# Own PSUM banks for two key and two query transposes, a third transpose buffer, a lag of three for the first eight units, and no steps put off

## The chip, the cores and the metric

One Trainium2 chip, of which one core runs the whole program. The metric is device time in microseconds (us) of one execution, the median of several executions. The engines are named as in the profile: PE (TensorE matmuls), PEld (TensorE weight loads), DVE (VectorE), ACT (ScalarE), POOL (GpSimd) and SP (SyncE, which here only issues transfers).

## What is computed

Attention with a position bias for 4 batches, 8 heads, 576 positions and a head size of 64, followed by a feed-forward block on the 2304 tokens (model size 512, hidden size 2048). Cut to what matters:

```python
scores = q @ k.transpose(0, 1, 3, 2) / sqrt(D)
psi_rel = log1p(abs(pos[:, None] - pos[None, :])); psi_i = log1p(maximum(pos[:, None], 1))
h = maximum((psi_rel / psi_i)[..., None] @ w1 + b1, 0.0)      # 32 hidden values per pair of positions
scores = scores + (h @ w2).transpose(2, 0, 1)[None]           # one bias for each head
attn = exp(scores - max(scores)); attn = attn / (sum(attn) + 1e-09)
x = (attn @ v).transpose(0, 2, 1, 3).reshape(B * S, H * D)
h = x @ w_in
out = (h / (1.0 + exp(-1.702 * h))) @ w_out
```

## The kernel before, in words

Every product of f32 operands is made of f16 halves: each operand is split into a high and a low part, and three products (high by high, high by low, low by high) are added in PSUM. The split of an operand is an ACT copy (high part) and a DVE or POOL subtraction (low part).

The attention runs in 72 units. A unit is one batch `b`, one chunk `c` of 128 query positions (the fifth chunk has 64) and one pair of heads `hp`. For unit `u` the main loop (line 655) writes down, in this order:

- `emit_s(u)`: the score products of both heads into one four-bank PSUM tile of the pool `ps_s` (line 329).
- `emit_soft1(u)`: bias added and maximum taken on DVE (line 352), exponential on ACT (line 359), split into `hl` (lines 364 to 367), and one transposing transfer `aT<-hl` on SP's queue (line 373). `a32` and `hl` have two buffers each, the target `aT` has two of tag `aT` for units up to 28.
- some steps of the feed-forward block, `msteps` (line 666).
- `emit_av(u - AV_LAG)`: the products of the transposed attention with V for an earlier unit, into a one-bank tile of the pool `ps_h` (line 392), then the scaling `xf` and split `xn`, and after the last head pair of a chunk the transposing transfer `xT<-xn` (line 426).
- weight conversions (`W_STEPS`, up to three per unit until all 32 are done), the first half of a bias step, more steps of the feed-forward block (line 667), the second half of the bias step, the bias load of unit `u + 2`, and what `todo` holds for the unit: loads, query transposes `trans_q`, key transposes `trans_k`, V splits.

`ps_s` has one buffer of four banks: score tiles, the tiles of `trans_q` (line 244), of `trans_k` (line 271) and of some bias steps follow one another in it. `ps_h` has two buffers of one bank, shared by `emit_av` and the first feed-forward product `hp` (line 488). `ps_o` has two buffers of one bank.

The feed-forward block works on ten blocks of tokens (both batches of a chunk; 256 tokens, or 128 for the fifth chunk), 16 steps each. A step is `emit_m1` (12 matmuls `hp<-xT,wi`, line 496, then ACT, DVE and POOL work) and, two steps behind, `emit_m2` (6 matmuls `op<-wo,gT`, line 525). A block's steps may be written down once the last of its units has had its `emit_av`; for the first block that is unit 10 of the loop. A unit has one step ahead of `emit_av` (`STEPS_A`) and one behind it (`STEPS_B`), except that `STEPS_B` is 0 in units 13, 15, 17, 19, 21 and 23. What is left is done after the loop (line 676).

The order written down is a priority, not the final order: a planner simulates the program at build time, and on each engine a step that is not ready in that simulation is passed by later ones. On the chip each engine and each transfer queue then works strictly in the order so found.

At the start, the last 64 key positions of batches 0 and 1 are loaded into two buffers of tag `xT` (lines 607 and 609), which later hold the transposed blocks `xT`.

Of the kernel before, what the change touches and what calls it, by code (L numbers as in the profile page):

```python
# [7 lines left out]
F32 = mybir.dt.float32  # L8
F16 = mybir.dt.float16
U32 = mybir.dt.uint32  # L10
ACTF = mybir.ActivationFunctionType
# [9 lines left out]
def kernel(  # L21
# [26 lines left out]
    nc = tc.nc  # L48
    B, H, S, D = q.shape
# [3 lines left out]
    NF = DFF // 128  # L53
    NP = H // 2
    SM = 512
    ST = S - SM
    BS = 512.0
    KS = 8.0
# [21 lines left out]

    W_AHEAD = 3
    BIAS_AHEAD = 2
    AV_LAG = 2
    STEPS_A = {}
    STEPS_B = {u: 0 for u in (13, 15, 17, 19, 21, 23)}
    W_STEPS = [1, 2, 2, 3, 3, 3, 3, 3, 3, 3, 3, 3]

    cst = ctx.enter_context(tc.tile_pool(name="cst", bufs=1))
# [2 lines left out]
    ps_s = ctx.enter_context(tc.tile_pool(name="ps_s", bufs=1, space=PSUM))  # L91
    ps_h = ctx.enter_context(tc.tile_pool(name="ps_h", bufs=2, space=PSUM))
# [4 lines left out]
    idn = cst.tile([128, 128], F32, name="idn")  # L97
# [17 lines left out]
    NU = len(units)  # L115
# [5 lines left out]
    for g in range(B // 2):  # L121
        b0, b1_ = 2 * g, 2 * g + 1
        for c in range(5):
            n = 128 if c < 4 else ST
# [3 lines left out]
    last_unit = [0] * len(blocks)  # L128
# [85 lines left out]
    q_st, k_st, kt_st, v_st = {}, {}, {}, {}  # L214
    qT, kT, v16 = {}, {}, {}

    def stage(shape, dt, tag, name):
        return wk.tile(shape, dt, tag=tag, name=name, bufs=BUFS[tag])

    def lo_part(on_pool, out, in0, scale, in1):  # L220
        if on_pool:
            nc.gpsimd.tensor_tensor(out=out, in0=in0, in1=in1, op=ALU.subtract)
        else:
            nc.vector.scalar_tensor_tensor(  # L224
                out=out, in0=in0, scalar=scale, in1=in1, op0=ALU.mult, op1=ALU.subtract
            )
# [11 lines left out]
        nc.sync.dma_start(out=t, in_=q[b, :, 128 * c:128 * c + n, :].rearrange("h p d -> p h d"))  # L238
        q_st[b, c] = t

    def trans_q(b, c):
        t = q_st.pop((b, c))
        n = t.shape[0]
        ps = ps_s.tile([128, 4, 512], F32, tag="s", name="qp")[:, 0, 0:NP * n]
        for hp in range(NP):
            nc.tensor.transpose(
                ps[:, n * hp:n * hp + n], t[:, 2 * hp:2 * hp + 2, :].rearrange("p a d -> p (a d)"), idn[:n, :n]
            )
        d = stage([128, 2, NP * 128], F16, "qT", "qT")[:, :, 0:NP * n]
        nc.scalar.activation(out=d[:, 0], in_=ps, func=ACTF.Copy, scale=QS)  # L250
        lo_part(False, d[:, 1], ps, QS, d[:, 0])
        qT[b, c] = d.rearrange("p x (u n) -> p x u n", u=NP)
# [16 lines left out]
    def trans_k(b, e):  # L269
        t = k_st[b, e]  # L270
        pair = ps_s.tile([128, 4, 512], F32, tag="s", name="kp").rearrange("p (u a) n -> p u (a n)", u=2)
        for u in range(2):
            ps, hp = pair[:, u, 0:S], 2 * e + u
            for c in range(4):
                nc.tensor.transpose(ps[:, 128 * c:128 * c + 128], t[:, u, c, :], idn)
            nc.tensor.transpose(ps[:, SM:S], kt_st[b][:, hp, :], idn[:ST, :ST])
            d = stage([128, 2, S], F16, "kT", "kT")
            nc.scalar.activation(out=d[:, 0], in_=ps, func=ACTF.Copy, scale=KS)
            lo_part(False, d[:, 1], ps, KS, d[:, 0])
            kT[b, hp] = d  # L280

    def load_v(b, e, tag="st"):

# [39 lines left out]
    s_ps, a_t, rs_t, aT = {}, {}, {}, {}  # L323
# [19 lines left out]
    def emit_soft1(u):  # L343
        bt = bt_t[u]
        at = wk.tile([128, 2 * S], F32, tag="a32", name="a32", bufs=BUFS["a32"])
        mx = wk.tile([128, 2], F32, tag="mx", name="mx")
        sm = wk.tile([128, 2], F32, tag="sm", name="sm", bufs=6)
        hl = wk.tile([128, 2, 2 * S], F16, tag="hl", name="hl", bufs=BUFS["hl"])
        for a in range(2):
            cs = slice(S * a, S * a + S)  # L350

            nc.vector.tensor_tensor_reduce(  # L352
                out=at[:, cs], in0=s_ps.pop((u, a))[:, 0:S], in1=bt[:, cs], scale=-1.0 / BS, scalar=3.0e38,
                op0=ALU.add, op1=ALU.min, accum_out=mx[:, a:a + 1],
            )
            nc.vector.tensor_scalar(  # L356
                out=mx[:, a:a + 1], in0=mx[:, a:a + 1], scalar1=LN_AS, scalar2=None, op0=ALU.add
            )
            nc.scalar.activation(  # L359
                out=at[:, cs], in_=at[:, cs], func=ACTF.Exp, scale=-1.0, bias=mx[:, a:a + 1],  # L360
                accum_out=sm[:, a:a + 1],
            )
            if a < VEC_EXP.get(u, 0):
                nc.vector.tensor_copy(hl[:, 0, cs], at[:, cs])
            else:
                nc.scalar.copy(hl[:, 0, cs], at[:, cs])  # L366
            (nc.vector if a and u in VEC_EXP_LO else nc.gpsimd).tensor_tensor(  # L367
                out=hl[:, 1, cs], in0=at[:, cs], in1=hl[:, 0, cs], op=ALU.subtract
            )
        rs_t[u] = sm  # L370

        t = stage([128, 18, 128], F16, "aT" if u <= max(BIAS_A) or u % 4 < 2 else "ht", "aT")
        nc.sync.dma_start_transpose(out=t, in_=hl.rearrange("p x n -> p (x n)"))
        aT[u] = t

    NXB = 2
    xT, x_n = {}, {}
# [97 lines left out]
    def weights_to(n):  # L475
        while w_done[1] < min(n, 2 * NF):
            split_w()
# [78 lines left out]
    def drain_to(j):  # L556
# [5 lines left out]
    FIRST = {1: (trans_k, 0, 0), 3: (trans_q, 0, 0)}  # L562
    SECOND = ((trans_q, 1, 0), (trans_k, 1, 0), (split_v, 0, 0))
    FIRST_UNITS = (
        (0, (load_k, 1, 1)), (1, (split_v, 1, 0)), (2, (trans_k, 0, 1)),
        (1, (load_v, 0, 1)), (4, (split_v, 0, 1)), (3, (load_v, 1, 1)),
        (4, (trans_k, 1, 1)), (6, (split_v, 1, 1)),
    )
    BIAS_A = {*range(4), *range(5, 21), 22, 24, 26, 28}
    BIAS_B = set(range(4))  # L570
# [2 lines left out]
    def at(u, fn, *args):  # L573
        todo.setdefault(u, []).append((fn, args))

    def put(us, items):
        assert len(us) == len(items)
        for u, x in zip(us, items):
            at(u, *x)
# [3 lines left out]
    for g in range(B // 2):  # L583
        b0, b1_ = 2 * g, 2 * g + 1
        o = g * UPG
        for c in range(4):
            put([o + 8 * c + x for x in (2, 5, 4, 7)], (
                (load_q, b0, c + 1), (trans_q, b0, c + 1), (load_q, b1_, c + 1), (trans_q, b1_, c + 1),
            ))
        if g + 1 < B // 2:  # L590
            n0, n1 = b0 + 2, b0 + 3
            for u, x in (
                (27, (load_kt, n0)), (28, (load_kt, n1)), (29, (load_k, n0, 0)), (30, (load_k, n1, 0)),
                (31, (load_v, n0, 0)), (32, (load_q, n0, 0)), (32, (trans_k, n0, 0)), 
                (32, (load_k, n0, 1)), (33, (load_q, n1, 0)), (33, (trans_k, n1, 0)), 
                (33, (load_k, n1, 1)), (33, (trans_q, n0, 0)), (34, (load_v, n1, 0)),
                (35, (split_v, n0, 0)), (35, (trans_q, n1, 0)), (35, (trans_k, n0, 1)),
                (36, (split_v, n1, 0)), (36, (load_v, n0, 1)), (36, (trans_k, n1, 1)), (37, (load_v, n1, 1)),
                (37, (split_v, n0, 1)), (38, (split_v, n1, 1)),
            ):  # L600
                at(o + u, *x)
# [12 lines left out]
        out=idn, in_=idn, compare_op=ALU.not_equal, fill=1.0, base=0, pattern=[[-1, 128]], channel_multiplier=1  # L614
# [16 lines left out]
    def bias_first():  # L631
        if bq:
            c, i = bq.pop(0)
            eng = BIAS_ENG[8 * c + i]
            half.append((c, i, eng, bias_hidden(c, i, eng, ("ht", "ht"))))

    def bias_second():
        if half:
            x = half.pop(0)
            bias_products(*x, "os")  # L640
            bdone[x[0]] += 1

    def bias_get(u):
        c = units[u][1]
        assert bdone[c] == (8 if c < 4 else 4)
        bias_load(u)

    def msteps(ready, n):
        n *= 256
        while n > 0 and fpos[0] < ready:  # L650
            n -= step()

    for u in range(BIAS_AHEAD):
        bias_get(u)
    for u in range(NU + AV_LAG):
        if u < NU:
            emit_s(u)
            emit_soft1(u)
        ready = NF * sum(1 for x in last_unit if x < u - AV_LAG)
        msteps(ready, STEPS_A.get(u, 1))  # L660
        if u >= AV_LAG:
            emit_av(u - AV_LAG)
        if u < len(W_STEPS):
            weights_to(w_done[1] + W_STEPS[u])
        if u in BIAS_A:
            bias_first()
        msteps(ready, STEPS_B.get(u, 1))
        bias_second()
        if u in BIAS_B:
            bias_first()  # L670
            bias_second()
        if u + BIAS_AHEAD < NU:
            bias_get(u + BIAS_AHEAD)
        for fn, args in todo.get(u, ()):
            fn(*args)
# [56 lines left out]
```

## Time and profile before

| what | value |
|---|---|
| median of 3 runs | 750.28 us (749.64 to 752.01) |
| the profiled execution's own time | 748.27 us |
| its span, first to last instruction | 746.4 us |
| mean granted TensorE clock | 0.93 of full speed |
| PE busy | 636.8 us (85% of the span) |
| DVE busy | 452.4 us (61%) |
| ACT busy | 421.2 us (56%) |
| POOL busy | 344.5 us (46%) |

The profile is of one execution; its span and the time around it (748.27 - 746.4 = 1.9 us) make its own time, which is 2.0 us under the median of the runs. Shares of busy time are means over stretches that have different limits, so the rows below are read stretch by stretch.

### The profile page before, as it was taken

To read this page: it belongs to the slowest core of one execution; us is meant where nothing else is said; L and a number is where in the kernel's file an instruction comes from. 1 tells how busy PE (TensorE), PEld (TensorE's weight loads), DVE (VectorE), ACT (ScalarE), POOL (GpSimd) and SP (SyncE) were. 2 spreads that over 40 slices of the span, in tenths; PEclk is the share of its full clock that TensorE was granted. 3 is DMA by queue.
4 is the path that set the end of the run, shared out by engine and by line. 5 is a ranking of instruction groups with operands and counts; after the bars stand their busy time and mean duration, and the time that the engine had idled before them with its cause. 6 is when DMAs were issued, how large, how long until landed. Compare 5 with 4: busy or idle time off the path is not lost.

```text
span 746.4 us, 17317 instructions
## 1 busy us (share of the span) xinstructions
PE 636.8 (85%) x6648; PEld 403.6 (54%) x6648; DVE 452.4 (61%) x1232; ACT 421.2 (56%) x971; POOL 344.5 (46%) x432
## 2 busy tenths in 40 slices
PE   5664763468988888999969899889999999999997
PEld 3222332235544555666647466566666666667665
DVE  6677769988556546645667566434676766642221
ACT  6899896577557745655445445763435454432133
POOL 2204634444445535655443465654474665552222
PEclk9778696569999999999998999999999999999999
DMA  9778989999867758877666676985467775752000
GB/s 241 227 256 233 289 189 220 259 239 242 184 148 144 171 104 168 170 153 145 145 145 144 154 137 124 199 160 117 86 135 145 160 143 124 143 102 54 1 29 15
DMA packets 249843, 116.50 MB, mean 156 GB/s; under 512 B 229792, under 2 KB 234016, under 8 KB 249760
## 3 DMA queue, kind: packets, MB, share of 16 engines
q1 hardware_dynamic: 241664, 99.38, 63.5%
q10 hardware_dynamic: 7952, 15.43, 5.9%
q8 instruction: 52, 0.85, 0.5%
q0 software_dynamic: 144, 0.59, 0.2%
q14 instruction: 31, 0.25, 0.1%
HBM read 52.85 MB, written 15.34 MB: 91 GB/s over the span
## 4 chain that ended last, share of the span: by engine, by line
PE 60%; DMA 14%; ACT 9%; DVE 9%; issue 4%; POOL 2%; SPq 1%; ACTq 0%; DVEq 0%; POOLq 0%
PE hp L496 22%; PE op L525 20%; DMA aT<-hl 11%; PE ot L404 7%; PE sp L336 5%; ACT a L359 3%; DVE a L352 3%; ACT ht L165 2%; PE ot L397 2%; POOL hl L367 2%; PE o L188 2%; ACT os L195 1%; DVE sm L388 1%; ACT hl L366 1%; ACT v L318 1%
## 5 line engine op out<-in xcount | busy, mean ns | idle before, releaser
L367 POOL TENSOR_TENSOR hl<-a,hl 128x576 f16<-128x576 f32 x142 | 189.1, 1344 | 123.0 <-ACT hl L366 59.6
L496 PE MATMUL hp<-xT,wi 128*128 128x256 f16 (+1 forms) x1920 | 219.5, 266 | 12.6 <-DMA xT<-xn 6.3
L525 PE MATMUL op<-wo,gT 128*128 128x512 f16 x864 | 216.8, 383 | 1.7 <-DVE gT L511 1.6
L496 PEld LDWEIGHTS <-wi 128*128 128x128 f16 x1920 | 170.5, 99 | 52.6 <-issue 16.9
L512 POOL TENSOR_TENSOR gT<-th,gT 128x256 f16<-128x256 f32 (+1 forms) x160 | 105.0, 657 | 165.1 <-DVE gT L511 89.8
L502 ACT ACTIVATE th<-hp 128x256 f32<-128x256 f32 (+1 forms) x160 | 57.2, 359 | 164.7 <-PE hp L496 156.0
L504 DVE SCALAR_TENSOR_TENSOR th<-th,hp 128x256 f32<-128x256 f32 (+1 forms) x160 | 62.4, 391 | 120.9 <-ACT th L502 120.9
L359 ACT ACTIVATE a<-a,mx 128x576 f32<-128x576 f32 x144 | 110.3, 768 | 42.2 <-DVE mx L356 41.8
L525 PEld LDWEIGHTS <-gT 128*128 128x128 f16 x864 | 81.0, 98 | 73.7 <-issue 3.9
L352 DVE CUSTOM_DVE_ANT_0 a<-sp,bt 128x576 f32<-128x576 f32 x144 | 103.1, 753 | 26.4 <-PE sp L336 22.6
L336 PE MATMUL sp<-kT,qT 64*128 64x512 f16 (+1 forms) x960 | 71.8, 297 | 13.7 <-DVE kT L224 3.6
L165 ACT ACTIVATE ht<-tab,pk 128x576 f32<-128x576 f32 x96 | 78.2, 863 | 5.8 <-PE ol L190 3.6
L404 PE MATMUL ot<-v,aT 128*128 128x64 f16 (+1 forms) x1920 | 78.8, 201 | 0.0
L404 PEld LDWEIGHTS <-aT 128*128 128x128 f16 (+1 forms) x1920 | 72.3, 106 | 3.7 <-issue 3.0
L366 ACT CAST hl<-a 128x576 f16<-128x576 f32 x103 | 66.0, 665 | 4.7 <-DMA aT<-hl 4.5
L419 POOL TENSOR_TENSOR xn<-xf,xn 128x128 f16<-128x128 f32 x72 | 35.4, 491 | 62.2 <-ACT xn L418 52.8
L397 PE MATMUL ot<-v,aT 128*128 128x128 f16 (+1 forms) x240 | 29.0, 233 | 39.1 <-DMA aT<-hl 39.0
L336 PEld LDWEIGHTS <-qT 64*128 64x128 f16 (+1 forms) x960 | 28.9, 99 | 56.5 <-issue 27.6
L388 DVE TENSOR_SCALAR sm<-sm 128x2 f32<-128x2 f32 x72 | 29.4, 408 | 35.9 <-ACT a L359 35.8
L188 PE MATMUL om<-ht,pk 128*32 128x512 f32 x152 | 41.5, 781 | 10.4 <-ACT os L195 10.4
L397 PEld LDWEIGHTS <-aT 128*128 128x128 f16 (+1 forms) x240 | 17.8, 104 | 58.0 <-DMA aT<-hl 47.0
L511 DVE CAST gT<-th 128x256 f16<-128x256 f32 x112 | 42.4, 379 | 4.4
(60 smaller groups left out, 562.9 us busy)
## 6 DMA issues: line engine op xcount, KB each, us to landing
bt<-scr SPq DMA_DIRECT2D x31, 576.0 KB, 4.4
scr<-os ACTq DMA_DIRECT2D x36, 288.0 KB, 4.1
w<-in_moe_w_in_dram SPq DMA_DIRECT2D x16, 512.0 KB, 5.3
w<-in_moe_w_out_dram SPq DMA_DIRECT2D x16, 512.0 KB, 5.2
k<-in_k_dram SPq DMA_DIRECT2D x32, 128.0 KB, 4.3
q<-in_q_dram SPq DMA_DIRECT2D x16, 256.0 KB, 4.8
out_dram<-ob ACTq DMA_DIRECT2D x16, 256.0 KB, 3.5
bt<-scr SPq DMA_DIRECT2D x8, 288.0 KB, 4.6
```

The costliest lines, as they stand in the source:

```text
L165: nc.scalar.activation(out=h, in_=tv, func=ACTF.Relu, bias=b1c, scale=sc[:, col:col + 1])
L336: nc.tensor.matmul(ps[a][64 * e:64 * e + m, cs], lhsT=qt[r, x, hp + e, 0:m], rhs=kT[b, hp + e][r, y, cs], start=i == 0, stop=i == 2,)
L352: nc.vector.tensor_tensor_reduce(out=at[:, cs], in0=s_ps.pop((u, a))[:, 0:S], in1=bt[:, cs], scale=-1.0 / BS, scalar=3.0e38, op0=ALU.add, ...
L359: nc.scalar.activation(out=at[:, cs], in_=at[:, cs], func=ACTF.Exp, scale=-1.0, bias=mx[:, a:a + 1], accum_out=sm[:, a:a + 1],)
L366: nc.scalar.copy(hl[:, 0, cs], at[:, cs])
L367: (nc.vector if a and u in VEC_EXP_LO else nc.gpsimd).tensor_tensor(out=hl[:, 1, cs], in0=at[:, cs], in1=hl[:, 0, cs], op=ALU.subtract)
L397: nc.tensor.matmul(o[po, 0:128], lhsT=t[:, 9 * y + 4, po], rhs=vt[:, x, 256:384], start=i == 0, stop=False, skip_group_check=True,)
L404: nc.tensor.matmul(o[po, 64 * a:64 * a + 64], lhsT=t[:, 9 * y + 5 * a + kb, po], rhs=vt[:, x, 384 * a + 64 * kb:384 * a + 64 * kb + 64], s ...
L496: nc.tensor.matmul(p[:, :n], lhsT=wi16[:, x, cc, 128 * f:128 * f + 128], rhs=r, start=i == 0, stop=i == 11,)
L504: nc.vector.scalar_tensor_tensor(out=g[:, :n], in0=th[:, :n], scalar=1.0, in1=p[:, :n], op0=ALU.add, op1=ALU.mult)
L512: nc.gpsimd.tensor_tensor(out=gt[:, 1, :n], in0=g[:, :n], in1=gt[:, 0, :n], op=ALU.subtract)
L525: nc.tensor.matmul(op_t[j, i], lhsT=gt[:, x, ts], rhs=wo16[:, f, y, :], start=f == 0 and n3 == 0, stop=f == NF - 1 and n3 == 2,)
```

## The change

`trans_q` gets a switch with which its tile comes from `ps_h` in place of `ps_s`; it is set for the two query transposes of units 5 and 7 (chunk 1, batches 0 and 1). A new function `trans_k_own` replaces `trans_k` in units 2 and 4 (head pairs 2 and 3 of batches 0 and 1): it transposes the last 64 key positions of both pairs first, into one `ps_h` tile, copies and splits them, and then handles each pair's other 512 positions in a `ps_h` tile of its own. The target of the attention's transposing transfer has the tag `xT` in units 2 and 5, so that three buffers serve the first units. The lag of `emit_av` is 3 in units 0 to 7 and 2 after that; unit 8 has two `emit_av` (5 and 6). `STEPS_B` is empty: units 13, 15, 17, 19, 21 and 23 have a step behind `emit_av` as well.

```diff
--- before.py
+++ after.py
@@ -80,9 +80,10 @@
 
     W_AHEAD = 3
     BIAS_AHEAD = 2
-    AV_LAG = 2
+    AV_LAG = {u: 3 for u in range(8)}
+    AT_X = {2, 5}
     STEPS_A = {}
-    STEPS_B = {u: 0 for u in (13, 15, 17, 19, 21, 23)}
+    STEPS_B = {}
     W_STEPS = [1, 2, 2, 3, 3, 3, 3, 3, 3, 3, 3, 3]
 
     cst = ctx.enter_context(tc.tile_pool(name="cst", bufs=1))
@@ -238,10 +239,14 @@
         nc.sync.dma_start(out=t, in_=q[b, :, 128 * c:128 * c + n, :].rearrange("h p d -> p h d"))
         q_st[b, c] = t
 
-    def trans_q(b, c):
+    def trans_q(b, c, own=False):
         t = q_st.pop((b, c))
         n = t.shape[0]
-        ps = ps_s.tile([128, 4, 512], F32, tag="s", name="qp")[:, 0, 0:NP * n]
+        if own:
+
+            ps = ps_h.tile([128, 512], F32, tag="h", name="qp")[:, 0:NP * n]
+        else:
+            ps = ps_s.tile([128, 4, 512], F32, tag="s", name="qp")[:, 0, 0:NP * n]
         for hp in range(NP):
             nc.tensor.transpose(
                 ps[:, n * hp:n * hp + n], t[:, 2 * hp:2 * hp + 2, :].rearrange("p a d -> p (a d)"), idn[:n, :n]
@@ -278,6 +283,28 @@
             nc.scalar.activation(out=d[:, 0], in_=ps, func=ACTF.Copy, scale=KS)
             lo_part(False, d[:, 1], ps, KS, d[:, 0])
             kT[b, hp] = d
+
+    def trans_k_own(b, e):
+
+        t = k_st[b, e]
+        tails = ps_h.tile([128, 512], F32, tag="h", name="kt")
+        ds = []
+        for u in range(2):
+            nc.tensor.transpose(tails[:, ST * u:ST * u + ST], kt_st[b][:, 2 * e + u, :], idn[:ST, :ST])
+        for u in range(2):
+            ds.append(stage([128, 2, S], F16, "kT", "kT"))
+            kT[b, 2 * e + u] = ds[u]
+            nc.scalar.activation(
+                out=ds[u][:, 0, SM:S], in_=tails[:, ST * u:ST * u + ST], func=ACTF.Copy, scale=KS
+            )
+        for u in range(2):
+            lo_part(False, ds[u][:, 1, SM:S], tails[:, ST * u:ST * u + ST], KS, ds[u][:, 0, SM:S])
+        for u in range(2):
+            ps = ps_h.tile([128, 512], F32, tag="h", name="kp")
+            for c in range(4):
+                nc.tensor.transpose(ps[:, 128 * c:128 * c + 128], t[:, u, c, :], idn)
+            nc.scalar.activation(out=ds[u][:, 0, 0:SM], in_=ps, func=ACTF.Copy, scale=KS)
+            lo_part(False, ds[u][:, 1, 0:SM], ps, KS, ds[u][:, 0, 0:SM])
 
     def load_v(b, e, tag="st"):
 
@@ -369,7 +396,7 @@
             )
         rs_t[u] = sm
 
-        t = stage([128, 18, 128], F16, "aT" if u <= max(BIAS_A) or u % 4 < 2 else "ht", "aT")
+        t = stage([128, 18, 128], F16, "xT" if u in AT_X else "aT" if u <= max(BIAS_A) or u % 4 < 2 else "ht", "aT")
         nc.sync.dma_start_transpose(out=t, in_=hl.rearrange("p x n -> p (x n)"))
         aT[u] = t
 
@@ -562,9 +589,9 @@
     FIRST = {1: (trans_k, 0, 0), 3: (trans_q, 0, 0)}
     SECOND = ((trans_q, 1, 0), (trans_k, 1, 0), (split_v, 0, 0))
     FIRST_UNITS = (
-        (0, (load_k, 1, 1)), (1, (split_v, 1, 0)), (2, (trans_k, 0, 1)),
+        (0, (load_k, 1, 1)), (1, (split_v, 1, 0)), (2, (trans_k_own, 0, 1)),
         (1, (load_v, 0, 1)), (4, (split_v, 0, 1)), (3, (load_v, 1, 1)),
-        (4, (trans_k, 1, 1)), (6, (split_v, 1, 1)),
+        (4, (trans_k_own, 1, 1)), (6, (split_v, 1, 1)),
     )
     BIAS_A = {*range(4), *range(5, 21), 22, 24, 26, 28}
     BIAS_B = set(range(4))
@@ -585,7 +612,8 @@
         o = g * UPG
         for c in range(4):
             put([o + 8 * c + x for x in (2, 5, 4, 7)], (
-                (load_q, b0, c + 1), (trans_q, b0, c + 1), (load_q, b1_, c + 1), (trans_q, b1_, c + 1),
+                (load_q, b0, c + 1), (trans_q, b0, c + 1, o + c == 0),
+                (load_q, b1_, c + 1), (trans_q, b1_, c + 1, o + c == 0),
             ))
         if g + 1 < B // 2:
             n0, n1 = b0 + 2, b0 + 3
@@ -652,14 +680,16 @@
 
     for u in range(BIAS_AHEAD):
         bias_get(u)
-    for u in range(NU + AV_LAG):
+    av = 0
+    for u in range(NU + 2):
         if u < NU:
             emit_s(u)
             emit_soft1(u)
-        ready = NF * sum(1 for x in last_unit if x < u - AV_LAG)
+        ready = NF * sum(1 for x in last_unit if x < av)
         msteps(ready, STEPS_A.get(u, 1))
-        if u >= AV_LAG:
-            emit_av(u - AV_LAG)
+        while av <= u - AV_LAG.get(u, 2):
+            emit_av(av)
+            av += 1
         if u < len(W_STEPS):
             weights_to(w_done[1] + W_STEPS[u])
         if u in BIAS_A:
```

## Rows read from the trace of the kernel before

**Rows 1.** Busy time of each engine by stretch (start:end in us, length, then engines).
```profile
core 0: us, PE busy (x) PEld busy (x) DVE busy (x) ACT busy (x) POOL busy (x), PEclk, DMA share, GB/s
36.00:60.00 24.00, 14.90 (x100) 5.08 (x99) 16.33 (x40) 22.33 (x45) 3.25 (x3) 0.81 0.78 257
60.00:141.00 81.00, 44.96 (x413) 22.62 (x413) 66.78 (x142) 63.20 (x122) 34.24 (x31) 0.75 0.97 237
141.00:156.00 15.00, 5.15 (x55) 2.83 (x55) 14.07 (x32) 10.88 (x21) 6.84 (x5) 0.61 0.99 231
...
184.00:300.00 116.00, 98.08 (x1037) 58.14 (x1036) 64.29 (x183) 70.94 (x148) 53.82 (x59) 0.94 0.75 156
...
480.00:680.00 200.00, 195.00 (x2181) 132.08 (x2178) 117.34 (x347) 91.91 (x244) 109.93 (x133) 0.99 0.65 130
680.00:746.00 66.00, 61.70 (x550) 42.43 (x547) 15.47 (x47) 16.74 (x51) 17.29 (x32) 0.99 0.07 20
```

**Rows 2.** What PE waited for, 36 to 160 us (total us, times, longest).
```profile
PE ot L397 <- DMA aT<-hl: 22.5, 7, 6.2
...
PE hp L496 <- DMA xT<-xn: 6.3, 1, 6.3
...
PE sp L336 <- DVE kT L224: 3.6, 2, 2.3
...
PE sp L336 <- DVE qT L224: 3.4, 2, 2.9
```

**Rows 3.** Timeline of PE and DVE, 62 to 114 us: transposes and scores in `ps_s`.
```profile
62.48 1.08 PE L275 MATMUL kp<-idn,k 128*128 128x128 f32 x4 [4.99 <-issue]
...
77.96 0.75 DVE L224 SCALAR_TENSOR_TENSOR kT<-kp,kT 128x576 f16<-128x576 f32 x1
...
79.45 0.91 PE L336 MATMUL sp<-kT,qT 64*128 64x512 f16 x12
...
90.33 1.12 PE L275 MATMUL kp<-idn,k 128*128 128x128 f32 x4
...
101.47 0.91 PE L336 MATMUL sp<-kT,qT 64*128 64x512 f16 x12 [1.29 <-DVE kT L224]
...
104.47 0.66 PE L246 MATMUL qp<-idn,q 128*128 128x128 f32 x4
...
113.45 0.91 PE L336 MATMUL sp<-kT,qT 64*128 64x512 f16 x12 [0.56 <-DVE qT L224]
```

**Rows 4.** Timeline of PE: first products of unit 7's AV, first feed-forward product.
```profile
141.31 0.50 PE L397 MATMUL ot<-v,aT 128*128 128x128 f16 x3 [3.68 <-DMA aT<-hl]
...
156.23 2.74 PE L496 MATMUL hp<-xT,wi 128*128 128x256 f16 x12 [6.32 <-DMA xT<-xn]
```

**Rows 5.** What PE waited for, 165 to 300 us, and two of the waits.
```profile
PE ot L397 <- DMA aT<-hl: 10.4, 6, 2.6
...
212.72 0.34 PE L397 MATMUL ot<-v,aT 128*128 128x128 f16 x3 [1.26 <-DMA aT<-hl]
...
267.18 0.50 PE L397 MATMUL ot<-v,aT 128*128 128x128 f16 x3 [2.43 <-DMA aT<-hl]
```

**Rows 6.** Groups by line over the span; transfers by issue (last row: us to landing).
```profile
L496 PE MATMUL hp<-xT,wi 128*128 128x256 f16 (+1 forms) x1920 | 219.5, 266 | 12.6 <-DMA xT<-xn 6.3 <-DVE th L504 4.3 <-DVE xf L411 1.8
L525 PE MATMUL op<-wo,gT 128*128 128x512 f16 x864 | 216.8, 383 | 1.7 <-DVE gT L511 1.6
...
L195 ACT ACTIVATE os<-ol,oc 128x64 f32<-128x64 f32 x19 | 5.8, 303 | 0.0
...
xT<-xn SPq DMA_TRANSPOSE x20, 3.1
```

**Rows 7.** Timeline around the start of block 6: PE, SP's queue, PE.
```profile
533.89 0.33 PE L397 MATMUL ot<-v,aT 128*128 128x128 f16 x3
...
541.44 1.26 SPq L426 DMA_TRANSPOSE xT<-xn  x1
...
555.84 1.47 PE L496 MATMUL hp<-xT,wi 128*128 128x256 f16 x12
```

## The prediction

> **What bounds the kernel now.** I read first the busy time of each engine by stretch [rows 1]. From 480 us on, PE is the bound: 195.0 of 200 us busy, and 61.7 of 66 behind 680. Work there costs what it costs; only idle PE time can be won back, and there is little of it. Ahead of 156 us it is otherwise: between 60 and 141 us PE is busy 45.0 of 81 us, DVE 66.8, ACT 63.2, and the DMA engines 0.97 of the time. No engine fills that stretch, several nearly do, so it is either a chain of waits or traffic that sets its length. Between them, from 184 to 300 us, PE is busy 98.1 of 116 us: 17.9 us idle.
>
> Then I read what PE waited for up to 160 us [rows 2]. The longest sum is the AV products' wait for the transposed attention: 22.5 us in 7 waits, so nearly each of the first eight units has one. Then comes one wait of 6.3 us for the first transposed block. The score products' waits for DVE's split of transposed keys and queries look small, 3.6 and 3.4 us, but they are only the ends of longer holds, because PE does other work during most of each hold. The timeline shows the holds themselves [rows 3]. `trans_k` of unit 2 enters the one four-bank buffer at 62.48 us; its second split starts at 77.96 and the score products of unit 3 start at 79.45, 17.0 us after the buffer was taken. `trans_k` of unit 4 takes it at 90.33 and unit 5's scores start at 101.47: 11.1 us. `trans_q` of unit 5 takes it at 104.47, unit 6's scores start at 113.45: 9.0 us. That is 37.1 of 81 us in which no score product could be made, whatever else was ready.
>
> The stretch ends with unit 7's AV at 141.31 and the first feed-forward product at 156.23 [rows 4]. Before 156 us PE has no feed-forward work; what comes earlier here moves all that follows, since what follows is mostly dense PE work.
>
> **The change part by part.** *Own banks.* The three holds of [rows 3], and a fourth in unit 7, leave the score buffer. The score products of units 3, 5, 6 and 8 can then follow the preceding maximum. The saving is not 37 us, because the work of that stretch remains: DVE 66.8 and ACT 63.2 us. With no hold at all it can't be shorter than 66.8 us, a gain of 14.2 us; if other waits take over, the gain is nothing. A single engine filled 22.33 of 24 us (93%) between 36 and 60 and 14.07 of 15 (94%) between 141 and 156 [rows 1]. Two engines that hand work to each other will stay below that. I take DVE at 90%: 66.8 / 0.90 = 74.2 us, so 6.8, say **-7.0 us**, ends 0 and -14.2.
>
> *The lag of three and the third buffer.* These are costed together with that gain: the waits of 22.5 us stand in PE's queue ahead of the next scores, and with three units of distance one more score product goes ahead of each. The third buffer is needed because a transposing transfer into one of two buffers would wait for an AV that is now later. It gets its place from the first key-tail tile, which the new function empties first. I cost that at nothing: the two tail transposes are the first PE work of the new function and come before the unit's transfer. If they were late, unit 2's transposing transfer would wait in SP's queue, and the weight, value and bias loads behind it too. The feed-forward work may still begin in unit 10; unit 8's double AV changes nothing in that.
>
> *Added instructions.* Each call of the new key function makes two copies of 64 columns more on ACT (303 ns for such a copy [rows 6]), while the other two get narrower by 64 columns; DVE likewise. For two calls this is between 0 and 4 x 0.303 = 1.2 us on either engine, and both are near their limit there: **+1.0 us**. PE makes the same transposes as before.
>
> *No steps put off.* A full step costs PE (219.5 + 216.8) us over 144 full steps (128, and 32 halves) = 3.03 us [rows 6]. Six steps, 18.2 us, leave the dense end and enter units 13 to 23. On a full PE that is nothing. But PE waits there: 10.4 us for transposed attention between 165 and 300 us, in six waits, of which four (1.26 the first, 2.43 the last, 7.5 together) stand right behind a place where a step was put off [rows 5]. A step of 3 us covers each. I take **-7.5 us**, ends 0 and -10.4. DVE (64.3 of 116) and ACT (70.9) have room for the steps' other work [rows 1].
>
> The put-off steps also bought something. With `STEPS_B` empty, units 10 to 17 hold exactly the 16 steps of block 0, and from then on each block is due as soon as it may be written down: no step is left in reserve. In the trace of before, block 6 shows what the reserve is worth [rows 7]. The last AV of its units starts at 533.89, its second transposing transfer is issued at 541.44 and lands some 3.1 us later (median [rows 6]), at 544.5. The block's first product starts at 555.84, so it had 11 us in hand, and between 533.89 and 555.84 PE did the six steps of reserve. Without them it is due near 535 and must wait until 544.5. In those 10.7 us PE has one step (3.0) and one more unit's scores and AV (about 0.9 each): 4.8 us of work and up to 5.8 us idle. I count five boundaries of this kind (blocks 2 and 5 to 8), so the ends are 0 and 29 us. The order is the planner's, which lets later scores and second products pass a step that isn't ready, so I take near the lower end, 1.2 us for each: **+6.0 us**.
>
> *Sum.* 748.27 - 7.0 + 1.0 - 7.5 + 6.0 = 740.8 us for an execution like the profiled one. That one lies 2.0 us under the median of the runs, so I forecast 742.8, rounded to **743 us**.
>
> **The rivals.** *The transfers are the bound.* The DMA engines are busy 0.97 of the stretch from 60 to 141 and 0.99 of the next [rows 1]. If that is work and not waiting inside the engines, earlier transposing transfers only slow the weight loads, which land later, and the stretch stays 81 us long. Against it: the rate there is 237 GB/s, while 36 to 60 shows 257 GB/s at a share of 0.78, so the busy share overstates the need. Time: 748.27 + 1.0 - 7.5 + 6.0 + 2.0 = 749.8 us, no change to speak of. The Trainium skill, "DMA: Bandwidth & Descriptors", section "Issuing engines are not separate DMA queues", says that transfers started by any engine end up on the same 16 DMA engines and interleave there, which is the mechanism of this rival; by it the time would be 749.8, by the reading of the rates above 743.
>
> *The missing reserve costs what it can* (the other side). Each of five boundaries leaves PE idle. For: PE has no slack in 480 to 680 us, the order is fixed at build time, and a first product that stands too early blocks all behind it. Against: where the planner sees the late transfer, it puts other work first. It decides from 13.5 / 5 = 2.7 us a boundary, where 7.0 - 1.0 + 7.5 is used up. At 4 us: 748.27 - 13.5 + 20 + 2.0 = 756.8 us; at the full 5.8: 765.8.
>
> *The first stretch falls to its floor* and the planner hides the boundaries: 748.27 - 14.2 + 1.0 - 7.5 + 2.0 = 729.6 us. For it speaks that 37.1 us of holds are removed where only 14.2 can be used. Against: ACT's and DVE's work is in a fixed order, and each is now and then ahead of the other.
>
> **How the numbers follow.** Chances: forecast 0.50 (735 to 747), floor 0.12, transfers 0.13, missing reserve 0.25. A measurement of this kernel tells about 0.3% (2.3 us) from no change. Faster by more: 0.50 + 0.12 = 0.62; within: 0.13; slower: 0.25. The range runs from the floor, 730, to the rival at 4 us a boundary, 757; I leave out about 0.06 below and 0.12 above. Likeliest time 743.
>
> **What would show it.** Right: unit 7's AV starts near 134 in place of 141.31 and the first feed-forward product near 149; score products no longer wait for DVE's splits; PE's wait for `aT` between 165 and 300 falls from 10.4 to about 3 us; the stretch behind the loop is about 18 us shorter. New: waits of PE for `xT` at later blocks, about 1 us each. Wrong: unit 7's AV still near 141 with DVE and ACT as idle as now (the holds were cover for transfers or for another wait), or waits for `xT` of 3 us and more at several blocks (the reserve), or SP's queue held by unit 2's transfer.

## The result, and the profile after

The changed kernel takes 741.92 us (median of 3 runs, 739.73 to 743.69) against 750.28: a ratio of 0.9894, with a 95% interval of 0.9859 to 0.9928. The forecast was 743. Its profiled execution took 739.73 us, with a span of 737.9.

The busy time of each engine by stretch, changed kernel (columns as in [rows 1]):

```profile
36.00:60.00 24.00, 16.07 (x124) 6.29 (x123) 21.16 (x55) 23.36 (x50) 3.69 (x3) 0.79 0.96 271
60.00:141.00 81.00, 49.04 (x430) 23.01 (x427) 76.23 (x153) 68.96 (x135) 37.98 (x35) 0.81 1.01 270
141.00:156.00 15.00, 8.13 (x79) 6.12 (x80) 13.79 (x30) 8.61 (x16) 4.33 (x4) 0.64 0.96 241
184.00:300.00 116.00, 105.94 (x1113) 65.78 (x1113) 68.55 (x186) 70.19 (x147) 52.99 (x61) 0.99 0.65 138
...
480.00:680.00 200.00, 191.60 (x2101) 128.91 (x2100) 117.25 (x339) 88.30 (x227) 106.39 (x126) 0.99 0.65 127
680.00:738.00 58.00, 52.81 (x491) 36.20 (x489) 12.78 (x39) 15.17 (x47) 14.61 (x28) 0.98 0.07 20
```

Against [rows 1], DVE does 4.8 us more in 36 to 60 and 9.5 us more in 60 to 141. PE does 7.9 us more in 184 to 300, and then gives 3.4 us back in 480 to 680. From 60 us to the start of unit 7's AV, before and after (same columns):

```profile
60.00:141.31 81.31, 44.96 (x414) 22.63 (x414) 67.08 (x142) 63.32 (x122) 34.55 (x31) 0.74 0.96 238
...
60.00:123.69 63.69, 41.31 (x372) 19.82 (x369) 59.57 (x126) 55.85 (x113) 32.92 (x32) 0.82 1.01 268
```

The timeline of the changed kernel, rows of PE, POOL and SP's queue:

```profile
11.50 0.43 PE L293 MATMUL kt<-idn,kt 64*128 64x64 f32 x2
...
25.41 0.60 PE L305 MATMUL kp<-idn,k 128*128 128x128 f32 x4
...
39.61 0.66 PE L305 MATMUL kp<-idn,k 128*128 128x128 f32 x4
...
123.69 0.50 PE L424 MATMUL ot<-v,aT 128*128 128x128 f16 x3
...
134.07 3.63 SPq L468 DMA_DIRECT2D w<-in_moe_w_in_dram  x3
...
134.14 0.87 POOL L446 TENSOR_TENSOR xn<-xf,xn 128x128 f16<-128x128 f32 x1
...
137.81 4.77 SPq L400 DMA_TRANSPOSE aT<-hl  x1
142.68 1.95 SPq L453 DMA_TRANSPOSE xT<-xn  x1
...
147.59 2.74 PE L523 MATMUL hp<-xT,wi 128*128 128x256 f16 x12 [7.54 <-DMA xT<-xn]
```

The same two steps in the kernel before, the block's last `xn` on POOL and the transfer `xT`:

```profile
147.67 1.01 POOL L419 TENSOR_TENSOR xn<-xf,xn 128x128 f16<-128x128 f32 x1 [4.03 <-ACT xn L418]
...
150.73 1.26 SPq L426 DMA_TRANSPOSE xT<-xn  x1
```

Unit 7's AV comes 17.6 us earlier than in [rows 4], the first feed-forward product only 8.6. Of the other 9 us, 5.6 are lost in SP's queue: the last `xn` is finished at 135.0, but `xT` is issued at 142.68, behind three weight loads and unit 9's transpose, 7.7 us later; before it was 2.1. It then lands after 4.9 us, against 5.5 before. Another 4.0 us lie between the start of the AV and the end of `xn` (11.3 us against 7.4). The first three rows of the changed kernel show what the prediction did not expect: the key transposes written down in unit 2, which stood at 62 to 69 us before [rows 3], are made at 11 to 40 us, before unit 0's AV.

PE's waits in the changed kernel, first 36 to 160 us (five rows), then 165 to 300 (two), then from 300 (one):

```profile
PE hp L523 <- DMA xT<-xn: 7.5, 1, 7.5
PE sp L363 <- DVE mx L379: 7.2, 3, 4.7
...
PE ot L424 <- DMA aT<-hl: 2.5, 2, 1.5
...
PE sp L363 <- DVE kT L225: 1.4, 1, 1.4
...
PE sp L363 <- DVE qT L225: 0.2, 1, 0.2
...
PE ot L424 <- DMA aT<-hl: 2.4, 3, 1.3
PE hp L523 <- DMA xT<-xn: 1.7, 1, 1.7
...
PE hp L523 <- DMA xT<-xn: 6.4, 5, 2.2
```

The wait for `aT` ahead of 160 us fell from 22.5 us [rows 2] to 2.5, those for DVE's splits from 7.0 to 1.6, and the one of 165 to 300 from 10.4 [rows 5] to 2.4. Part of this went over to other waits: ahead of 160 us the score products now wait 12.6 us for DVE's `mx` (two rows, 7.2 and 5.4, the longer one shown) where they waited 3.2, and all waits of PE listed there add up to 47.5 us against 57.4. New are six waits for `xT` at later blocks, 8.1 us in all. From the last AV to the end it is 53 us in place of 66, so 13 us less where the prediction said about 18.

### The profile page after: what moved, and what is told of

It reads as the page before. It is cut to its first block, busy times and chain, and to the rows that moved or that the text cites. A ratio compares the mean times of both kernels' runs of the same rounds, so it can differ in the third digit from the quotient of the medians.

```text
span 737.9 us, 17316 instructions
## 1 busy us (share of the span) xinstructions
PE 637.0 (86%) x6648; PEld 400.7 (54%) x6648; DVE 461.2 (63%) x1236; ACT 422.0 (57%) x975; POOL 341.9 (46%) x432
## 4 chain that ended last, share of the span: by engine, by line
PE 52%; DMA 17%; DVE 14%; ACT 9%; issue 5%; POOL 2%; SPq 1%; ACTq 0%; POOLq 0%; DVEq 0%
PE hp L523 19%; PE op L552 18%; DMA aT<-hl 9%; PE ot L431 6%; PE sp L363 4%; DVE a L379 4%; ACT a L386 3%; DMA xT<-xn 2%; PE ot L424 2%; ACT ht L166 2%; DMA scr<-os 2%; PE o L189 1%; DVE hl L391 1%; DMA out_dram<-ob 1%; DVE w L493 1%
## 5 line engine op out<-in xcount | busy, mean ns | idle before, releaser
L394 POOL TENSOR_TENSOR hl<-a,hl 128x576 f16<-128x576 f32 x142 | 187.0, 1326 | 138.7 <-ACT hl L393 68.0
L523 PE MATMUL hp<-xT,wi 128*128 128x256 f16 (+1 forms) x1920 | 215.4, 263 | 20.9 <-DMA xT<-xn 15.7
L363 PE MATMUL sp<-kT,qT 64*128 64x512 f16 (+2 forms) x960 | 75.0, 299 | 22.4 <-DVE mx L379 7.2
L431 PE MATMUL ot<-v,aT 128*128 128x64 f16 (+1 forms) x1920 | 77.0, 198 | 0.0
L431 PEld LDWEIGHTS <-aT 128*128 128x128 f16 (+1 forms) x1920 | 70.0, 104 | 3.7 <-issue 3.6
L538 DVE CAST gT<-th 128x256 f16<-128x256 f32 x112 | 45.6, 410 | 3.9
L445 ACT CAST xn<-xf 128x128 f16<-128x128 f32 x70 | 20.6, 294 | 43.0 <-DVE xf L438 41.6
L415 DVE TENSOR_SCALAR sm<-sm 128x2 f32<-128x2 f32 x72 | 24.0, 334 | 32.7 <-ACT a L386 32.5
L424 PE MATMUL ot<-v,aT 128*128 128x128 f16 (+1 forms) x240 | 28.6, 230 | 16.7 <-DMA aT<-hl 9.8
```

Of the source, the lines that this page charges most:

```text
L363: nc.tensor.matmul(ps[a][64 * e:64 * e + m, cs], lhsT=qt[r, x, hp + e, 0:m], rhs=kT[b, hp + e][r, y, cs], start=i == 0, stop=i == 2,)
L431: nc.tensor.matmul(o[po, 64 * a:64 * a + 64], lhsT=t[:, 9 * y + 5 * a + kb, po], rhs=vt[:, x, 384 * a + 64 * kb:384 * a + 64 * kb + 64], s ...
L523: nc.tensor.matmul(p[:, :n], lhsT=wi16[:, x, cc, 128 * f:128 * f + 128], rhs=r, start=i == 0, stop=i == 11,)
```

## The experiments

Every edit makes the planner plan again, so each run below changes one thing in the text of the kernel and possibly many in the order. A difference between two runs can thus also belong to the one plan that was found. "Put off" means that the six units have no step behind `emit_av`, as in the kernel before. Ratios are to the kernel before, run on the same chip.

| run | own banks | lag 3 | third buffer | steps | us, median | ratio (95%) |
|---|---|---|---|---|---|---|
| changed kernel | yes | yes | yes | not put off | 741.92 | 0.9894 (0.9859 to 0.9928) |
| 1 | yes | yes | yes | put off | 738.92 | 0.9866 (0.9837 to 0.9896) |
| 2 | no | no | no | not put off | 744.98 | 0.9961 (0.9938 to 0.9985) |
| 3 | yes | no | no | put off | 753.73 | 1.0069 (1.0041 to 1.0096) |
| 4 | no | yes | yes | put off | 749.48 | 1.0022 (1.0000 to 1.0045) |
| 7 | yes | yes | no | not put off | 742.15 | 0.9908 (0.9875 to 0.9942) |
| 8 | yes | no | yes | not put off | 741.30 | 0.9892 (0.9849 to 0.9936) |
| 9: run 3, one step moved | yes | no | no | put off | 737.04 | 0.9825 (0.9792 to 0.9857) |
| 10 | yes | no | no | not put off | 742.12 | 0.9898 (0.9860 to 0.9935) |

**Runs 1 to 4: the parts.** The first theory: own banks give most of the gain, and the steps come out near nothing.

```diff
 run 1, on the changed kernel
-    STEPS_B = {}
+    STEPS_B = {u: 0 for u in (13, 15, 17, 19, 21, 23)}
 run 2: the same lines the other way, on the kernel before
 run 3: run 1 and
-    AV_LAG = {u: 3 for u in range(8)}
-    AT_X = {2, 5}
+    AV_LAG = {}
+    AT_X = set()
 run 4: run 1, and all transposes back in ps_s (trans_k for trans_k_own, own=False)
```

> The changed kernel, but with the six steps of units 13 to 23 put off again. Theory (the whole gain comes ahead of the first feed-forward product; what the six steps fill in units 13 to 23 is paid back as waits for xT at later blocks): same as the changed kernel, 742 us within 2, the first feed-forward product near 147.6 us, PE's waits for aT between 165 and 300 us back to about 8 us, PE's waits for xT behind the first block back to nothing. Rival (the gain comes from the steps): 748 us or more.

> The kernel before with STEPS_B empty and nothing else changed. Theory: no change, 750 us within 2; first feed-forward product at 156 us as before, waits for xT of 1 to 2 us at five or six later blocks. Rival (the gain comes from the steps): about 742 us.

> The kernel before with the own banks for the two key and the two query transposes alone (lag two, two transpose buffers, steps put off). Theory (the holds of the score buffer were the wait, and the key transposes, no longer queued for that buffer, are planned ahead of the loop): most of the gain, 744 us (742 to 747), unit 7's AV before 130 us. Rival (the lag is what counts): 749 us or more, unit 7's AV near 141 us.

> The kernel before with the lag of three and the third buffer alone (shared banks, steps put off). Theory: little, 748 us (746 to 752), because the score products of units 3, 5, 6 and 8 are still held up by the transposes; unit 7's AV near 139 us. Rival (the lag is what counts): about 742 us, unit 7's AV near 125 us.

Run 1 keeps the whole gain, so the six steps are not needed for it. Run 2 gains a little by itself (0.4%), where none was expected. Run 4, lag and third buffer alone, gains nothing, although its unit 7's AV (149.20) and its first product (162.36) come later than before and than expected. But the theory fell with run 3: own banks alone are slower, although the timeline has unit 7's AV and the first product just where the prediction put them (134 and 149):

```profile
67.32 0.34 PE L424 MATMUL ot<-v,aT 128*128 128x128 f16 x3 [1.04 <-DMA aT<-hl]
...
69.49 0.33 PE L293 MATMUL kt<-idn,kt 64*128 64x64 f32 x2
...
133.67 0.50 PE L424 MATMUL ot<-v,aT 128*128 128x128 f16 x3 [2.71 <-DMA aT<-hl]
...
149.07 2.71 PE L523 MATMUL hp<-xT,wi 128*128 128x256 f16 x12 [3.52 <-DMA xT<-xn]
```

So those two points are no measure of the end, as run 4 shows from the other side. Busy time of run 3 from 156 to 184 us and from the start to 200, 300 and 680 us shows where it went; below it are the same rows of the kernel before:

```profile
156.00:184.00 28.00, 21.73 (x222) 12.97 (x221) 27.93 (x63) 21.40 (x43) 14.82 (x12) 1.00 1.03 246
...
0.00:200.00 200.00, 133.08 (x1175) 67.15 (x1176) 158.15 (x354) 155.73 (x309) 75.15 (x94) 0.81 0.96 239
0.00:300.00 300.00, 219.21 (x2064) 119.70 (x2064) 211.50 (x508) 215.48 (x434) 120.27 (x143) 0.85 0.86 207
0.00:680.00 680.00, 579.56 (x6072) 360.78 (x6073) 438.60 (x1189) 403.30 (x922) 325.62 (x399) 0.92 0.76 169
```

```profile
156.00:184.00 28.00, 26.04 (x265) 16.79 (x266) 23.97 (x57) 19.70 (x40) 12.40 (x12) 0.91 1.01 248
...
0.00:200.00 200.00, 125.39 (x1151) 65.51 (x1153) 153.33 (x341) 153.01 (x298) 73.78 (x91) 0.80 0.95 238
0.00:300.00 300.00, 209.92 (x2048) 115.56 (x2050) 209.23 (x501) 214.47 (x426) 119.50 (x141) 0.85 0.87 207
0.00:680.00 680.00, 575.11 (x6104) 361.14 (x6105) 436.98 (x1186) 404.48 (x921) 327.19 (x400) 0.92 0.76 169
```

Read the counts of PE, which do not depend on the clock, as the work done (both kernels show 6648 in all). Run 3 is 24 matmuls ahead at 200 us, 16 at 300, and 32 behind at 680. Matmuls are not alike (a mean of 383 ns for one of `op` [rows 6], 200 ns for the 64-column ones of AV), so I also weighed each kind with its busy time per matmul in the kernel before. By this estimate run 3 is 3.8 us ahead at 200 us, 2.7 at 300, and 3.8 behind at 680; its span ends 3.3 us later. From 156 to 184 its DVE is full (27.93 of 28 us), and PE does 43 matmuls fewer than before. From 300 to 680 PE is busy 4.8 us less than before (differences of the rows).

**Runs 5 and 6: is the early part bound by DVE's work or by transfers?** The second theory was that DVE's total work sets the first 190 us; the prediction's rival was that transfers do. Run 5 leaves two of the three bit operations out of each weight conversion; run 6 loads only every second weight tile and converts it twice. Both are edits of the kernel before and serve the measurement alone.

```diff
 run 5, split_w
-        nc.vector.scalar_tensor_tensor(out=w, in0=lo, scalar=29, ...)
-        nc.vector.scalar_tensor_tensor(out=w, in0=hi, scalar=0xC0000000, ...)
 run 6, load_w
+        if w_done[0] % 2:
+            w_st[w_done[0]] = w_st[w_done[0] - 1]
+            w_done[0] += 1
+            return
```

> The kernel before, with two of the three bit operations of each weight conversion left out (of the 64-bit words only the first shift is kept); loads and everything behind the conversion stay. Some 1.57 us of VectorE for each of 32 tiles, 33 us of them before 141 us. Theory that VectorE's work bounds the first 190 us: the first feed-forward product, at 156 us before, comes 8 us or more earlier, the last weight is done by 175 us in place of 187, and the time is 740 us or less. Rival that transfers bound the stretch: these points move by under 3 us, the transfer engines stay at 0.95 or more from 60 to 200 us, and the time is 746 to 751 us.

> The kernel before, with every second weight tile not loaded (two conversions read one loaded tile), so 16 of 32 transfers of 512 KB are left out; VectorE's work is the same. 8.4 MB fewer at about 250 GB/s are 33 us of transfers less in the first 190 us. Rival that transfers bound the stretch: the first feed-forward product comes 8 us or more earlier than 156 us and the time is 740 us or less. Theory that VectorE bounds it: under 4 us earlier, VectorE at 90% of 100 to 141 us as before, 745 to 750 us.

Run 5 took 745.99 us (ratio 0.9976, 0.9953 to 0.9999), run 6 746.64 (0.9964, 0.9937 to 0.9992). Run 5, busy time from 60 to 141 us, and its first feed-forward product on the timeline:

```profile
60.00:141.00 81.00, 41.64 (x369) 22.31 (x369) 39.84 (x94) 61.06 (x117) 26.07 (x29) 0.70 0.86 228
```

```profile
163.69 2.72 PE L490 MATMUL hp<-xT,wi 128*128 128x256 f16 x12 [3.19 <-DMA xT<-xn]
```

The same two of run 6:

```profile
60.00:141.00 81.00, 49.06 (x417) 23.70 (x417) 64.14 (x131) 64.58 (x123) 31.78 (x30) 0.78 0.78 194
```

```profile
155.69 2.72 PE L500 MATMUL hp<-xT,wi 128*128 128x256 f16 x12 [1.80 <-DMA xT<-xn]
```

Neither is the bound by itself. DVE's busy time dropped from 66.8 [rows 1] to 39.8 us, and the first product came 7.5 us later. The transfer engines' share dropped from 0.97 to 0.78, and it came half a microsecond earlier. The Trainium skill, "Perfetto Trace Analysis", section "Identifying the Most-Contended Engine", says to find the engine with the highest occupancy and to optimize it first; from 60 to 141 us that was DVE [rows 1], and with its busy time there down by 40% the kernel gained 0.24%, so run 5 does not bear the advice out here. The same section's advice not to go by the occupancy of the 16 DMA engines agrees with run 6 (0.97 to 0.78, and no earlier product to speak of). Whether ACT (63.2 us there), or DVE and the transfers together, set the length was not tried.

**Runs 7 and 8: what moved the key transposes?** The third theory: the third buffer pulls them ahead.

```diff
 run 7, on the changed kernel
-    AT_X = {2, 5}
+    AT_X = set()
 run 8, on the changed kernel
-    AV_LAG = {u: 3 for u in range(8)}
+    AV_LAG = {}
```

> The changed kernel without the third buffer (the transposed probabilities of units 2 and 5 go back to the aT buffers); own banks, the later attention-value products and the six steps stay as changed. Theory: the third buffer is what pulls the key transposes of the second pair ahead to 11 to 40 us, since it makes unit 2's target wait for a tile of theirs. Without it they fall to 70 to 80 us, as in the run with own banks alone, VectorE has less done in 36 to 60 us (16 us in place of 21), unit 7's attention-value products begin at 130 us or later, and the time is 748 us or more. Rival: the banks or the lag moved them; then they stay at 11 to 40 us and the time stays at 739 to 743 us.

> The changed kernel with all attention-value products two units behind; own banks, third buffer and the six steps as changed. Theory: the key transposes stay ahead, at 11 to 40 us, and most of the gain stays: 740 to 745 us, with some 3 to 6 us more of TensorE waiting for the transposed probabilities before 141 us. Rival: the lag itself carries the gain, and the time returns to 748 us or more.

It fell too. Without the third buffer the transposes stay early (`kt` at 11.46 us) and so does the time. Without the lag they go back to 69.39 us. Yet run 8 keeps its time, since its steps are not put off (run 10).

**Run 9: their place.** In run 3 the `kt` row follows unit 0's AV by 2.2 us. Both take `ps_h` buffers, which are handed out in the order written down. With a lag of two, unit 0's AV is written in unit 2, ahead of that unit's key transposes; with a lag of three it is written in unit 3, behind them. The fourth theory: the lag gains only through this order, which makes these transposes early ("early keys": at 11 to 40 us; "late": from 69 us on). Run 9 gives run 3 the order without the lag.

```diff
-        (0, (load_k, 1, 1)), (1, (split_v, 1, 0)), (2, (trans_k_own, 0, 1)),
+        (0, (load_k, 1, 1)), (1, (split_v, 1, 0)), (1, (trans_k_own, 0, 1)),
```

> Own banks alone as in the run that was 0.7% slower (lag of two throughout, no third buffer, the six steps put off), with one step moved: the key transposes of batch 0's second pair are written down in unit 1 in place of unit 2, so they come ahead of unit 0's attention-value products in the order in which the ps_h buffers are handed out. Theory: the lag of three gains because it gives the key transposes this place; here they go to 11 to 40 us without the lag, VectorE has 20 us or more done in 36 to 60 us, unit 7's attention-value products begin at 120 to 126 us, and the time is 736 to 743 us. Rival: the greater distance of the attention-value products is itself what gains; then the keys come early, PE waits for the transposed attention before 141 us as before, and the time stays at 748 to 754 us.

The time went from 753.73 to 737.04 us, the fastest kernel here. Its timeline and busy times:

```profile
11.33 0.34 PE L293 MATMUL kt<-idn,kt 64*128 64x64 f32 x2
...
130.63 0.50 PE L424 MATMUL ot<-v,aT 128*128 128x128 f16 x3 [4.24 <-DMA aT<-hl]
...
142.51 2.72 PE L523 MATMUL hp<-xT,wi 128*128 128x256 f16 x12 [5.06 <-DMA xT<-xn]
```

```profile
36.00:60.00 24.00, 14.24 (x119) 5.81 (x121) 20.63 (x55) 23.00 (x49) 3.53 (x3) 0.83 0.94 264
...
0.00:200.00 200.00, 136.68 (x1236) 70.43 (x1238) 162.45 (x357) 156.75 (x311) 81.56 (x95) 0.84 0.94 241
0.00:300.00 300.00, 221.61 (x2167) 121.27 (x2167) 219.25 (x525) 222.03 (x447) 129.83 (x148) 0.89 0.86 213
0.00:680.00 680.00, 586.48 (x6208) 367.95 (x6209) 442.84 (x1198) 406.47 (x929) 334.12 (x405) 0.94 0.76 170
```

It is 85 matmuls ahead of the kernel before at 200 us, 119 at 300 and 104 at 680 (by the estimate with weights 11.2, 15.3 and 12.1 us), and it ends 10.2 us earlier in span (746.4 - 736.2). Unit 7's AV came at 130.63, later than expected (120 to 126); as in run 3, that point told little. DVE did 20.63 us in 36 to 60, as expected, against 15.74 in run 3; how this early work becomes the time gained later is not shown step by step. Run 3 and this run were timed on different chips, each against the kernel before.

**Run 10: own banks and steps.**

```diff
 on the changed kernel
-    AV_LAG = {u: 3 for u in range(8)}
-    AT_X = {2, 5}
+    AV_LAG = {}
+    AT_X = set()
```

> Own banks and no steps put off; lag of two throughout, no third buffer. The key transposes stay late (70 us and later). Theory: the six steps fill PE between 200 and 300 us whatever the third buffer does, so this is 740 to 745 us, as the same kernel with the third buffer was (741.3). Rival: the third buffer carries that gain; then this stays at 749 us or more.

As expected: with own banks and late keys, the six steps alone turn run 3's 1.0069 into 0.9898.

What sets run 3 apart from runs 9 and 10 is best seen from 184 to 300 us, in this order:

```profile
184.00:300.00 116.00, 99.31 (x1017) 60.82 (x1016) 64.21 (x181) 65.72 (x139) 52.35 (x58) 0.90 0.69 148
...
184.00:300.00 116.00, 100.93 (x1100) 60.38 (x1098) 66.70 (x190) 75.29 (x159) 55.40 (x62) 0.99 0.73 163
...
184.00:300.00 116.00, 108.23 (x1136) 67.41 (x1136) 72.78 (x197) 68.17 (x146) 54.94 (x64) 0.99 0.72 152
```

PE is nearly as busy in run 3 as in run 9, yet does 83 matmuls fewer, at a granted clock of 0.90 against 0.99 (means between the two levels, 1.2 and 2.4 GHz; 0.94 before [rows 1], 0.99 in the changed kernel). In run 3 PE was busy 1.20 us of 224 to 228, and from 228 to 232 the granted clock was 0.50, the lower level. So against run 9, run 3 loses little there to idle time (16.7 us against 15.1) and more to the lower clock. No run tests the clock by itself.

**Runs 11 and 12: more of it, and without the banks.** Run 11 moves the other pair's key transposes (unit 4 to unit 2) as well, on run 1. Run 12 makes run 9's move in the kernel before, where the transposes use `ps_s`.

```diff
 run 11
-        (4, (trans_k_own, 1, 1)), (6, (split_v, 1, 1)),
+        (2, (trans_k_own, 1, 1)), (6, (split_v, 1, 1)),
 run 12
-        (0, (load_k, 1, 1)), (1, (split_v, 1, 0)), (2, (trans_k, 0, 1)),
+        (0, (load_k, 1, 1)), (1, (split_v, 1, 0)), (1, (trans_k, 0, 1)),
```

> The version with own banks, lag of three, third buffer and the six steps put off (738.92 us), with the key transposes of batch 1's second pair also written down in unit 2 in place of unit 4. Theory: they too go ahead, to 30 to 60 us in place of 74 to 82, the score products of units 4 and 5 come earlier, and the time falls by 1 to 4 us, to 735 to 738. Rival: VectorE is already full there (21 of 24 us in 36 to 60), the earlier splits delay unit 0 to 2 by what they give units 4 and 5, and the time is 738 to 742.

> The kernel before with one step moved: the key transposes of batch 0's second pair written down in unit 1 in place of unit 2, still in the one four-bank score buffer. Theory: the place pays only with the own banks; in the score buffer the transposes stand between the scores of units 1 and 2, which must pass through the same buffer, so they come at 45 us or later, unit 2's scores are held in place of unit 3's, and the time is 745 to 752 us. Rival: the place alone is the gain; then the keys come well before 45 us, unit 7's attention-value products begin at 120 to 128 us, and the time is 737 to 742 us.

Run 11: 741.84 us (0.9898, 0.9865 to 0.9931). Those transposes did go to 40.16 us, and nothing was gained over run 1, as the rival of the expectation said. Run 12: 756.82 us (1.0090, 1.0058 to 1.0122). Its timeline:

```profile
50.12 1.01 PE L336 MATMUL sp<-kT,qT 64*128 64x512 f16 x12
...
55.79 1.12 PE L275 MATMUL kp<-idn,k 128*128 128x128 f32 x4
...
63.02 1.12 PE L275 MATMUL kp<-idn,k 128*128 128x128 f32 x4 [4.59 <-DVE kT L224]
...
69.05 0.91 PE L336 MATMUL sp<-kT,qT 64*128 64x512 f16 x12
```

Unit 1's scores, the two transposes and unit 2's scores pass through the one score buffer in turn, 18.9 us from one score product to the next. The place pays only with the own banks. It cost more than I expected (745 to 752).

## Why the prediction was right, point by point

The time and the sign came out. Of the sum's terms, those for the steps and the reserve came out near their size as waits of PE, the one for own banks did not last to the end by itself, and the lag, which had no term of its own, moved work that I had not followed.

- **Own banks, -7.0 us.** Taken alone (run 3) they moved the first product by 7.2 us, as forecast, and cost 0.7% in the end. The step that failed is the sentence "what comes earlier here moves all that follows, since what follows is mostly dense PE work": the 24 matmuls gained by 200 us were gone by 680. DVE full from 156 to 184 us goes with a loss there, but run 10 has the same (27.90 of 28 us, PE 216 matmuls) and gains in the end. From 184 to 300 the clock was lower. Between 300 and 680 run 3 lost 48 matmuls against before: the 36 of two feed-forward steps, and most of the others from AV. PE's listed waits behind 300 us add up to 20.7 us against 14.5, in ten kinds of which none but AV's wait for `aT` is above 3 us (5.9, and 6.1 before); so no single wait explains it, the order there is a new plan, and the cause stays open. Own banks with late keys and the steps put off is this one plan; how much of its loss is the plan's own is not known.
- **The floor of -14.2 us** for that stretch was no floor. Unit 7's AV moved by 17.6 us. I had taken the stretch's work as fixed, but DVE did 59.6 us of work between 60 us and that AV in place of 67.1, since 4.8 us of it lay ahead of 60 and the rest behind the AV. And DVE was busy 94% of that time, against 83% before and the 90% that I took.
- **The lag and the third buffer, "costed together with that gain".** This is the other step that failed. The distance of the AV products and the third buffer are worth nothing that can be told (runs 7 and 9). But the lag changed which step comes first in `ps_h`, and with the steps put off that is what makes own banks pay: 1.0069 without it, 0.9866 with lag and third buffer, 0.9825 with the order alone. All five plans with own banks and early keys (the changed kernel, runs 1, 7, 9 and 11) lie between 0.9825 and 0.9908. The written order was at hand in the code and I did not follow it through the buffers. It is one of two ways to the gain: with late keys, own banks pay when the six steps are not put off (0.9898, run 10, against 0.9961 for the steps alone). The changed kernel has both and is no faster than with either; why they don't add was not tried.
- **Added copies, +1.0.** The four narrow copies take 0.7 us on ACT and 0.7 on DVE in all, and half of them now lie at 36 to 39 us. No run shows a cost.
- **Six steps, -7.5.** The wait they were to cover fell by 8.0 us (10.4 to 2.4); in run 1, where they are put off, it is 9.8. The prediction counted idle time only; the granted clock of 184 to 300 us rose too, from 0.94 to 0.99.
- **The reserve, +6.0.** The waits at block boundaries are there: 8.1 us in six waits, against five of 1.2; run 1 has none of them. Together the two come to +0.1 us where -1.5 was forecast. What the six steps do to the end depends on the rest: -0.4% alone (run 2), -1.7 points with own banks and late keys (run 3 to run 10), and with early keys 738.92 us put off against 741.92 not put off, with ratios whose intervals overlap.
- **Rivals.** Transfers as the bound: run 6 speaks against it. The rule beside it, from the Trainium skill, "DMA: Bandwidth & Descriptors", section "Issuing engines are not separate DMA queues", was not tested by itself; what run 6 speaks against is that this sharing sets the length of the stretch. The missing reserve is real but costs 1.4 us a boundary, below the 2.7 from which it decides. The floor's time (729.6) was not reached by any run.

So the forecast's total rests partly on luck: the part that I sized was lost later, and a part that I did not see brought it back.

## What to carry to other kernels

Where a planner or a pool hands out buffers in written order, ask of each step moved to a new pool, and of each lag changed, what it now stands ahead of and behind in that pool; moving one line was worth 2.4 points here. An earlier milestone is not an earlier end: count the bound engine's finished work at several later times, kind by kind, and read the granted clock beside it. Before calling a stretch bound by a busy engine or by transfers, take some of that work away and look whether anything moves.

## What the hardware showed that was not expected

PE's busy time is no measure of its work: from 184 to 300 us, 99.31 us of it held 1017 matmuls in run 3 and 100.93 us held 1100 in run 9, at granted clocks of 0.90 and 0.99. Over the whole span the mean clock does not order it either: 6648 matmul records take 636.8 us before (0.930), 637.0 in the changed kernel (0.954) and 644.5 in run 3 (0.929). And in a stretch of 81 us in which DVE was busy 82% and the transfer engines 0.97 ([rows 1]), neither was the bound by itself: with 40% of DVE's busy time there gone, or half of the weight transfers, the kernel gained 0.2% to 0.4%.
